# Fewer idle TensorE products at both ends of a Conformer block, and a new order of its blocks and PSUM banks

## The chip, the cores and the metric

One core of a Trainium2 chip runs the whole program. The metric is the device time of one execution in microseconds; three executions are taken and their median counts.

## The reference

A Conformer block over `x` of 2 x 4000 x 144 in bfloat16, with 4 heads of 36:

```python
h = layernorm(x);  x = x + 0.5 * (silu(h @ w_ff1a) @ w_ff1b)       # 144 -> 576 -> 144
h = layernorm(x);  q, k, v = split(h @ w_qkv)                      # 4 heads of 36
x = x + softmax(q @ k.T / 6) @ v @ w_o                             # over all 4000 keys
h = layernorm(x) @ w_pw1;  h = h[:, :144] * sigmoid(h[:, 144:])
x = x + silu(depthwise_conv5(h)) @ w_pw2                           # 5 taps along time
h = layernorm(x);  x = x + 0.5 * (silu(h @ w_ff2a) @ w_ff2b)
return layernorm(x)
```

## The kernel before

The 8000 tokens are cut into 16 chunks of 500, eight per sequence; a chunk is four blocks of 125 tokens. For each chunk of queries the keys come in 63 tiles of 64. A tile's scores (`PS<-QT,KT`, four products of 500 columns) go to two PSUM banks, ScalarE exponentiates both in one instruction (`PT<-PS`, 128 x 1000), and four products `PS<-PT,VA` add the result to banks 6 and 7. Some tiles are exponentiated on VectorE by integer arithmetic instead. Around this stream go, for each chunk, the first feed-forward, the projections, and after attention the output projection, the gated convolution and the second feed-forward. In the middle of the program a sigmoid or silu is a tanh on ScalarE (`TH`) and a product on VectorE (`HT`, `U`, `SW`); in the front and in the tail silu is taken directly. A layer norm is statistics on VectorE (`ST`), a power -0.5 on GpSimd (`RS<-RS,NHALF`), and the scaling (`XN`) on GpSimd in the middle and on VectorE at both ends. Normed rows are transposed to `XT` or `XTQ` by DMAs through memory in the middle, and by TensorE products with `IDENT` and a copy at both ends.

Three stages matter for reading the profile. The front runs chunk 0 in two halves (`pre_first`) up to the first exponential, with chunk 1 beside it. In the middle, attention of all chunks runs against the rest. The tail begins when the last tile of chunk 15 is exponentiated: chunk 15's attention is finished (`epilogue`, copies to `QT`, products with `IDF`, `AN`), and then it and what is left of chunks 11 to 14 go through `post1`, `post2` and the last layer norm (`store`), in halves of 250 tokens.

The program is made in two steps. Generators ask for work and a planner (`Sched`, `pick_any`) emits instructions through `Rec.op`, with planned durations, which fixes what is computed and in which tile. Then `reorder` permutes the blocks of each engine by the table `ORDER`, one character per block (how far the block is shifted in its engine's queue), and `place` takes each PSUM tile's bank from `PLACES`. Semaphores are set after that. Each engine runs its queue strictly in this order.

An idle product is a 128 x 128 product of the identity with itself into bank 7 (`warm`). The program starts with `NWARM = 50` of them. Further ones are put in by `Rec.op`: in the front up to the first exponential, and in the tail, when the planner finds that a TensorE instruction will wait for another engine, it fills the planned wait:

```python
            for _ in range(int((ready - start - 0.12) / 0.056)):
                self.filler()
```

They belong to the block of the instruction that waits, and move with it. Nine such waits of the front got 5, 2, 5, 29, 6, 1, 5, 2 and 1 of them, five of the tail 6, 14, 6, 15 and 9. All instructions are issued by one helper, so every row of the profile has line L377; rows are told apart by their tiles.

Of the kernel before, what the change touches and what calls it, by code (L numbers as in the profile page):

```python
# [32 lines left out]

ALPHABET = '!#$%&()*+,-./0123456789:;<=>?@ABCDEFGHIJKLMNOPQRSTUVWXYZ[]^_`abcdefghijklmnopqrstuvwxyz{|}~'
ORDER = {
    "pe": (
        "PPPPPPPPQOPPPRRRNLPPQSPROQQQHTOPPMRPRMQNV[NZMMMtMKPMOLIOOOQNQORRNTYLVESPPKLRPEEOOOQNPP[PNQNNQOMPP^PP"
        "JPNPNQ[TLNKMQOKPNSQMNUOOOROSPPQXRGNPROUQYHKNNPNPNQQMPPPQOPWXNNNNPMM]]MNNOMQNLQLMMPPPTOOOOPPPQOUOOOOO"
        "TWQWQKLJQNRPWITNNVOLLOORNOQOSYNNPMZNNNOMOOVN[PMSJPLQKQSQWQXHRWRVQRYWRHXR=BRALJRTMVOLWTLMPMPUUHOWORLO"
        "VOOROOBPPQOUPQMPRUQRTLQTQDPIPPQQQQQUQQHMRVOLRNNNPPPTOOOOPPPPQOROQRVOVPQMNPTROWQSLOUNOPXOUROMVMNZOS-R"  # L40
        "MKMOOOQOPQXQOLOOOOOXOOOPNOOOXOOOPNQNTMTOMNXNPNP_OLNQOLRNNN]OMRMOUKVMNYQMRPQHTYCMOLOWOMNNOROQLQOPTOOO"
        "ORROQLPVOOOOOUNOPPQQKPPPPPPPROSPRLTMTNNNOROOUORNORLORPQQSKO[_PYQRNOIFINLTLNNQNPSSNTMMYQNRRSMMSNUOCUP"
        "NYOVPROOJORRTNS>NNPTTOMNNUOOORNNTOOOOXROQSPPSQGXPPPPVOOOTROUSPPUQGPP3PPPQOPPPQRNOSOPXPPQOPVPQRPKBWSO"
        "OQNJOPZPNRNNNQQ]MQOQHPMSPPMKPPPPP^UOOPKMQRLQLRLNVPXMNNQMMTNNROMQQNURNOWRPMIQNNPPRRSNPKPPPPQQNPPPPPUP"
        "PPPQYIOOOOTNNOMRPRRVSPLXNSSMNTUOTJNTRMR8MPQSSOLQQTKQNNSPVMQMNOQNTQSMRNRJOUOOPNOQTNPSSLYLMRRMM]PNQIPM"
        "ORTMSOKQJSSSOSVJRPHPKPQOQOUPNOOQNPQRNOPPSOPNSOSQSQKRPRSOFRRMRMOSQSMRRKMRPNRUSMOTKMPTM_TRLMNQOPRSQMMW"
        "TOOOORO:VPNOOOOPQOPQOQOPROOPPPVOPQOWKPUOKOOVQOIOOOPPPPSOSOPRUQQHLXPPPQOVP_FLNNTMPNWZMPMGLMUMPNLOPQOP"
        "QOPQQURTNJOTROINSOOOQOTOOOQXMOOOPXMNNOOOOOPROOPPQOPPPPPPPPQOPPPPQSPUWQWIKPWJPJQVPQRKSNRfNPPQSSMNNb8R"
        "MMMRLMSMNQSLUN_ZOKNPN>TOLLMRLNQOSQOMPROURPNWO_HNNNNPPLOYNPRRKKPKSPMRN`RMQMMRSMMQNVVNVPXLNPRR@NSVO[NO"
        "OSNOVPMPNPTROSQSZROSQT(EOTJMOSQSNSJNSSPLULOO]NPMWNOOPKMNVMOOSNUMTLNNSMOTXMNNNOPNO]PNOTQNLMNOOORTQMMO"  # L50
        "PQRPSPPQUSGPTQQWQQUQTNCCMRPYPLOOSOOLRMOPPQ]QMNQOWOKNOMNRPRVJNRPMMQOURTMNLNSPSQLWROURPVZQTQTRW?ERAQGQ"
        "QQWPPPPPUBQULMVPNKQNNROOPPVPPXLPYRKOJOROOVPPEOPNPPeRORLOPTOPNUQMNCNNORNQMQQNRRNSQRNUQHQULPLSNPZPK[NO"
        "MPNRKNPKQNPPXOOSNNOMOPVOOOOPNROOPPPPQOPPPPQQNWPPPPPPTHPNOUOROMNQOROOSOPNPQOPQOQOSO`NP[LNOQLYQKPSINSP"
        "RFFPQQNQOPQOPQOUPPPPTPSOOQRPTWQNNWOP;MOOOPVOOOOOXNOO[PMOTTMOHLMO]OOOQNNOSPPMKQOPPSSOOLPPPPSPPQLPPPPQ"
        "OWOWNPMMNNQQRLOPPPPROOPQOPPPPQOPPPTPPSOUOIVNNNYNTMPNOXOWGOWPPULPIEQQLPURNQNSKOOPQOROOPWOQOQOPQVPUFNO"
        "WN_JNNNNNOOQNNOSNPQQQJPXOUNOOOSWMOGVORLNLQRMSPPLPPPRPSMOORPSQOKROOQUPTZOO_RPNEGNOSLNNNOU]MNNNNOPNXOP"
        "LMOPNOPQOPPVOOQOMWNRRMMULNSNOQLQOPRXOPQOPQOG[OOOOOPNTNNNNPQXNOOPPMXQRSXPSLRWEEORPHdLOPQOLcVNLOPTOSHJ"
        "NL[DNOMQMQOKPQRLWPTLNPNLPQOPPP]TOMUNLOLOMOOPPPPPQOSUPMQOKPPROQRPTROINQQQSXKOMOOOOOP]OOQNNOOUNNNO]LQN"
        "NOOOOO]NNQMNUNNNNNNRPNSOOOPWOOOOOTNNOOWOOOOOOOPPPPROSNOQSPLOYOOOTNNOWNPURHOLVKOXPNLPPPROQQGPQOPQQNQQ"
        "QQQKQQWURYZMTQMESHOLCQORSUSOKKQSLPQMQUNRNNRPUQJNURNSKMNRTNVRcMTINRSNSFNO[FOQLMMSOLXMMPVMPMMPTLXUMMQL"  # L60
        "MVLXMNOMRUNNJORNOPQSSXOMJPPPXKPM[PMOOROU_GXKLMVJMMMMTLTLMTMPMOZOOSNNOMOOOPPPRRTTTPNRSTRFNQTAOPNQOPTO"
        "OPNPPQOPPPPPQQRSQRRIWQTQTTEVKVRJRNRKYPP>WNOMNNNRNSNOOQOPZPNVNPPLPKQLP]ROMNOTQNLQNRSVNGNOOOPQOQTRMNRP"
        "YPJPQUNPNOQGWPRMOVLOPSKNSMOOQOPSOOTRMOMPTRPNRPVQOPQOUPUXNQMSQK:RLRROVKQRPLSKOOPSOPRPLPPPPPUOPNOOPPPP"
        "UOPQMRMOQXPMQNNQNNPQOPPPXQNQMNPNRNOPSPNVNOOOOTPPUSPMOTPTUUNLSMNSPP:YOOOQQMMPNPUSNOMRRLUROKNSQRSKPKRO"
        "OVOUNNNNQQLQQNQQQQLSOOOPPSOOYTOLNWPLUKMPRUSQOIRPDQOQOPPRROMPROOQQN"
    ),
    "act": (
        "PPPPPPPPPPPPQRSMNOPRPQQQKPPQOPQOPUOOOOOPPPRPQSQUNIVSSNORIIPPPPPPPPPPPPPQOPPQOPPPPPPPPQOPPPPPPPPPPPPP"
        "PPQOPPPPPPPPPPPPPPPPPPPPPPPPPPPPPPPPPPPPPPPPPPPPPPPPPPPPQOPPPPPPPPPPPPROOROQNPQOPPPPPPPPPPPPPPPPPQOP"
        "QQNPPQOPPPPPPPPPPPPPPPPPPPPPPPPPPQOPPQOPPPPPPPPPPPPROOPPPPPPPPPPPPPPPPPPQOPPPPPPPPPPPPPPPPPPPQOPPPPP"  # L70
        "PQOQOPPPPPPPPQOPPPPPPPPPPPPPPPPPPPPPPQOPPPPPPPPPPPPPPPPPROQNQQQMQOPPPPPPPPPPPQOPPPPPPPPQOPPPPPPPPPPP"
        "PPPPPPPPPPPPPPPPPSOOOPPPPPPPPPQOPPPPPPPPPPPPPPPPPPPQQNPPPPPPPPPPQQNPPQOPPQOPQOQOPPPPPPPPPPPPPPPPPPPP"
        "PPPPPPPPPPQOPPPPPPPPPPPPPPPPPPPPPPPPPPQOPPQOPPPPPPQOPPPPPPPPPPQOPPPPPPPPPPPPPPPPPPPPPPPPPPQOPQOPPPPP"
        "QOQOPPQOPPPQOPPPPPPPPPPPPPPPPPPPPPPPPPPPPPPPQQNPPPPPQOPPPPPPPPPPPPPPPPPPQOPPPPPPPPPPPPPPPPPPPPPPPPPP"
        "PPPPPPPPPPPPPPPPPPPPPQOPPPPPPPPPQOPPPPPPPPPPPPPPPPPPPPPPPPPPPPPPPPPPPPPPPPPPPPPPPPPPPPPPPPPPPPPPPPPQ"
        "OQOQOPPPPPPPPPPPPPPPPPPPPPPPPPPPPPPPPPPPPPPPPPPPPPPPPPPPPPPPPPQOPPPPPPPPPPROOPPQOPPPPPPPPPPQOPPPQOPP"
        "PPPPPPPPPPPQOPPPPPPQOPPPPPPPPPPPPPPQQNPPPPPPPPPPPQOPQOPPPPPPQOPPPPPPPPPPPPPPPPPPPPPPPPPPPPPPPPPPPQOP"
        "PPPPPPPPPPPPPPPPPQOPPPPPPQOQOPPPPPPPQOPQOQOPPPPQOPPQQQMPPPPTOOUQMMOUVMORSSMIJPPPPPQQQMPPPPPPQO"
    ),
    "dve": (  # L80
        "PPQOQQQMPPQOaOOOOQR`MNJNOPLRNNYYHPMKOPJRNQJQQNRROQQQQIUPUPNSSSTGSSSTFSFRSSURUICZJSLOLPVOPNIXNNORNNPM"
        "QQNPQOPQOPPPROOPPPPQOPPPPPPPQOQOPPPQRPQRPQQTPQRRSLPRRTRURUQRURRSTRSWSQRUQUUPQTT#US2T3NSQpTROORPQR?OC"
        "SOMRPQmQINPGMNNNNNNOMPNOOOPNPPPPPPSQSNPQXPPQRRMRMR9QNQOPQOPPPPPPPPPPWPNPNOPNPRRNTPLPQQTPQORPVPPPPP@P"
        "PPQOPQOPROOROQNROOROOcOOOOOOOPNQNNOOOOOOQOQQVMVPNOKNOQOPPSTTOSOJQRHQSQTRPUUWQSGCKKOPPPPPUPTPPRVIPPPR"
        "ORTRNRNSP=WNPNOPNOPUQNPRLNPPPPP_OPNOQNPPLO]NNOMOOPNOOSQMQLQOPPQRNRNQNVPQOQOJPPPQOPPPQOTOTOOLOQQQQQSS"
        "PSSPKRPBRPNPPPQOPQOPPPPQQNPQSNRNQTQOPVQOFOTOMOOQOQQNQQRROQRIRNQXQRNRRMRURRORHRROQ<QRPRROJSPRSQKQQQTP"
        "SOOaRBNNQNNPNOPNOOOOQOROOROOPPQOQOTOOOO_OOPRPLPPPROOGQNPQQNPZPNPQMNPPPLPPPPQOPPPPPPQQNPPPQOPPPQOPTRO"
        "SQSQSJPFPPPROOUQOPPQUQTNORDMQOQOPQQNQSPSLNOPQOPPPPQRPTRKRRRKTPSORRMRPSPTQNRSQSQTJP5O`PPPPPPPPPPEOOPN"
        "PROOQOQOQOPPQOQOQOPQOPPPSPPQLPQRNRNSNPNPROOQOPQQRMOQOPPPPPPPPPPPROOPQSPPQQQIPPPPPPROOPPPRPNTPNPQQLPP"
        "PPROOPRPNQRNOPROOQOQQNROOPPQOQRNQQMQOQQNQQNPPQOPPPQOPRORPMPSOOOQOQOPQUPPUOOPPQSQDNSOOOPPPPPPQQRPRPRP"  # L90
        "RPREORPNPPPSOOOPROQNPPPPPPPROOQQNQOPPQOPPPPPQRNOQQNPPPPPPPPPPQQRMRPSLOUNTQMMMPPPPPPPPPPPPPPPPPPPPPPP"
        "PPROQQQLQTNOOOPPPPPQOQOUPQMPQLPROQRMSNSNNOPPPPPPPPPPPPUPNQNNSOOOPPYOOOOOOOOOQOPRORSQRMQIPPPPRRRMRLOP"
        "PPPPPQOPPPPPPPQOQOROOROQNPPPPPQOQOPPPPPPPPPPPPPPPPPPQOQOPQOPPPQOPROOPPPSOOOPPPPPQOPPPROQTMSORLSLOOPQ"
        "OPPP_OQOROKROLSMNNNPPPPPPPPPPPPQUQMPPRPRPQGPSOORNOPQOQOTPNPSPLOQOSQNTMOPNRROMQOSQRMRLQNPQOPPPPPQQQSQ"
        "SNROQQEPPPPPPPPWPPPQOPRPQFQOPPPPPPQOQOPPPPTQSMMNPPPQRNOSOSOMQRMSNUOMSNRMRLQNQRNOQOQQNPPRSOSOPRRRRTLQ"
        "SQAQQRPHPPQOPPROOROOPPSOOSPPQQQQQQSPPRTRN?NPPPROSNPSPPQTRSNRRLCRPQMPROQNPROQNPPPRRNNPPQOPPUOQOROQXPH"
        "PNOOYbTLNOOXPSPUQQSACFQRUSUSTBUWZQR^SSKCMBO=OPPMORSTNQXQQHPPQOF"
    ),
    "pool": (
        "PQQQQSSOORPQTQOPQQTQQNQQQQQRRORPQQQQQ,PXOOOOOOO_NORNSMMNNOOQNNPWSNNOMPQQQKTTNNNNQQNPPPROTPMTOPTKNROQ"  # L100
        "QKPWOOOOOPNPQOPPSOOQNPPQOPQQN"
    ),
    "sp": (
        "PPPPPPPPQOPPPPPPPPPPPROQSMRNNPPPPPPPPPPPQOQOPPPPWOVNNNNNNPPPPPPRRNNRRNNPPPPPPPPRRNNPPZOOXNOMNNNNNVOO"
        "OO[NNWNNNNNNNNT[NNNNOOOOVNNXMNNNOOOOP[OOPNOOOPPPLPPPQO"
    ),
}
PLACES = (
    "5024031421242530124140023035304230343105232504015043214352103245041522040241204124012401314032034023"
# [40 lines left out]
class Rec:  # L150
# [22 lines left out]
    def op(self, eng, name, *a, r=(), w=(), q=None, cost=0.1, kind=None, lat=None, acc=None, bub=(0.0, 0.0), **k):  # L173
# [27 lines left out]
        start = ready = self.free[eng]  # L201
# [3 lines left out]
        if eng == "pe" and self.filler is not None and not self.filling:  # L205
            self.filling = True
            start = max(start, self.filler_free())
            for _ in range(int((ready - start - 0.12) / 0.056)):
                self.filler()
# [197 lines left out]
class Banks(Slots):  # L407
# [7 lines left out]
    keep = 0  # L415
# [1655 lines left out]
```

## Time and profile before

| | |
|---|---|
| median of three executions | 887.04 us (886.72 to 887.05) |
| the profiled execution | 887.44 us, span 885.6 us from the first to the last instruction |
| ScalarE, TensorE, VectorE, GpSimd busy | 851.5, 857.2, 818.4, 303.9 us |
| first exponential starts | 19.75 us |
| last exponential ends | 847.36 us |
| last TensorE instruction, last VectorE instruction end | 878.6 us, 881.1 us |
| DMA | 28.8 MB, mean 33 GB/s |

Each engine has a queue of its own, and times are from the span's start. In the timeline, `x4` is a run of four like instructions merged into one row with the start of the first and the time to the end of the last; the bracket gives the idle time before it and what ended it. A TensorE product's end is modelled and includes its way through the array (some 0.17 us), so the next row starts before the end of the last. PEld is the loading of weights. `L377` is the helper that issues everything.

### The profile page before, as it was taken

To read this page: it belongs to the slowest core of one execution; us is meant where nothing else is said; L and a number is where in the kernel's file an instruction comes from. 1 tells how busy PE (TensorE), PEld (TensorE's weight loads), DVE (VectorE), ACT (ScalarE), POOL (GpSimd) and SP (SyncE) were. 2 spreads that over 40 slices of the span, in tenths; PEclk is the share of its full clock that TensorE was granted. 3 is DMA by queue.
4 is the path that set the end of the run, shared out by engine and by line. 5 is a ranking of instruction groups with operands and counts; after the bars stand their busy time and mean duration, and the time that the engine had idled before them with its cause. 6 is when DMAs were issued, how large, how long until landed. Compare 5 with 4: busy or idle time off the path is not lost.

```text
span 885.6 us, 27130 instructions
## 1 busy us (share of the span) xinstructions
PE 857.2 (97%) x11478; PEld 385.1 (43%) x11478; DVE 818.4 (92%) x1799; ACT 851.5 (96%) x1095; POOL 303.9 (34%) x584
## 2 busy tenths in 40 slices
PE   8999999999999999999999999999999999999996
PEld 7544333444444434344344444443434343444466
DVE  7968999999999999999988899997988999999987
ACT  6799999999999999999999999999999999999974
POOL 7761500216235235024107125241631017022733
PEclk9999999999999999999999999999999999999999
DMA  4231011112211111212101111002011001101101
GB/s 101 45 61 36 23 37 31 34 23 44 44 30 23 37 30 27 47 24 43 23 19 28 30 32 29 22 17 51 22 37 24 7 15 45 29 9 36 37 17 34
DMA packets 114222, 28.81 MB, mean 33 GB/s; under 512 B 101085, under 2 KB 114100, under 8 KB 114100
## 3 DMA queue, kind: packets, MB, share of 16 engines
q1 hardware_dynamic: 112642, 26.46, 13.7%
q8 instruction: 90, 1.47, 0.7%
q10 hardware_dynamic: 1458, 0.62, 0.3%
q14 instruction: 32, 0.26, 0.1%
HBM read 13.44 MB, written 13.61 MB: 31 GB/s over the span
## 4 chain that ended last, share of the span: by engine, by line
ACT 43%; PE 39%; DVE 14%; POOL 1%; DMA 1%; SPq 1%; issue 1%; DVEq 0%; POOLq 0%
ACT PT L377 39%; PE PS L377 39%; DVE PT L377 8%; ACT TH L377 4%; DVE ST L377 1%; DVE HT L377 1%; DVE X L377 1%; POOL XN L377 1%; DVE QT L377 1%; DVE XN L377 1%; DVE KT L377 1%; SPq L377 1%; DMA XTQ<-rows 1%; POOL RS L377 0%; DVE VA L377 0%
## 5 line engine op out<-in xcount | busy, mean ns | idle before, releaser
L377 ACT ACTIVATE PT<-PS 128x1000 bf16<-128x1000 f32 (+1 forms) x822 | 756.3, 1066 | 5.0 <-PE PS L377 3.8
L377 PE MATMUL PS<-QT,KT 64*64 64x500 bf16 x3968 | 425.6, 385 | 14.0 <-ACT PT L377 8.3
L377 PE MATMUL PS<-PT,VA 64*37 64x500 bf16 x4712 | 410.8, 372 | 2.0 <-DVE PT L377 0.7
L377 DVE TENSOR_SCALAR PT<-PS 128x500 int16<-128x500 f32 x372 | 244.6, 669 | 8.0 <-PE PS L377 6.5
L377 PEld LDWEIGHTS PS<-QT,KT 64*64 64x64 bf16 x3968 | 124.5, 104 | 240.3 <-ACT PT L377 135.5
L377 POOL TENSOR_SCALAR RS<-ST 125x4 f32<-125x4 f32 x130 | 35.2, 271 | 459.9 <-DVE ST L377 453.7
L377 PEld LDWEIGHTS PS<-PT,VA 64*37 64x37 bf16 x4712 | 141.2, 96 | 96.4 <-DVE PT L377 20.7
L377 POOL TENSOR_SCALAR XN<-X,RS 125x144 bf16<-125x144 bf16 x260 | 153.0, 622 | 8.0 <-DMA out_dram<-XN 1.3
L377 DVE TENSOR_SCALAR PT<-PT 128x1000 uint16<-128x1000 uint16 x372 | 150.6, 416 | 1.9 <-PE PS L377 0.5
L377 DVE TENSOR_TENSOR PT<-PT 128x1000 bf16<-128x1000 bf16 x186 | 126.5, 682 | 1.4
L377 ACT ACTIVATE TH<-PS 128x500 bf16<-128x500 f32 (+3 forms) x198 | 105.1, 554 | 4.0 <-PE PS L377 2.7
L377 POOL TENSOR_TENSOR RS<-RS,NHALF 125x4 f32<-125x4 f32 (+1 forms) x93 | 91.5, 987 | 36.2 <-DVE RS L377 30.4
L377 DVE SCALAR_TENSOR_TENSOR HT<-TH,PS 128x500 bf16<-128x500 bf16 (+1 forms) x135 | 80.8, 617 | 17.7 <-ACT TH L377 16.9
L377 PE MATMUL PS<-XT,WA 128*128 128x500 bf16 (+4 forms) x288 | 74.9, 365 | 0.4 <-DVE AN L377 0.2
L377 DVE BATCH_NORM_STATS2 ST<-X 125x6 f32<-125x288 bf16 x160 | 65.6, 446 | 3.1 <-DMA X<-in_x_dram 2.9
L377 DVE SCALAR_TENSOR_TENSOR X<-PS,X 125x288 bf16<-125x288 f32 (+1 forms) x128 | 57.2, 451 | 9.7 <-PE PS L377 8.6
L377 PE MATMUL PS<-WB,HT 128*125 128x144 bf16 (+1 forms) x640 | 51.9, 230 | 0.6 <-ACT HT L377 0.4
L377 PEld LDWEIGHTS PS<-WB,HT 128*125 128x125 bf16 (+1 forms) x640 | 44.2, 136 | 14.0 <-issue 4.6
L377 POOL COPY U<-U 128x2 bf16<-128x2 bf16 (+1 forms) x54 | 12.0, 260 | 71.4 <-DVE U L377 71.4
L377 PEld LDWEIGHTS PS<-XT,WA 128*128 128x128 bf16 (+1 forms) x288 | 21.2, 97 | 34.0 <-issue 12.5
L377 PE MATMUL PS<-U,DG 128*128 128x375 bf16 (+6 forms) x204 | 29.0, 264 | 0.2 <-DVE PT L377 0.2
L377 DVE STREAM_TRANSPOSE XN<-XN 128x320 f32<-128x320 f32 x54 | 27.0, 500 | 1.7 <-POOL XN L377 1.6
(93 smaller groups left out, 533.3 us busy)
## 6 DMA issues: line engine op xcount, KB each, us to landing
rows<-XN SPq DMA_DIRECT2D x216, 40.0 KB, 2.0
XT<-rows SPq DMA_DIRECT2D x56, 128.0 KB, 2.0
rows<-AN SPq DMA_DIRECT2D x60, 40.0 KB, 2.0
X<-in_x_dram SPq DMA_DIRECT2D x16, 140.6 KB
XTQ<-rows SPq DMA_DIRECT2D x26, 70.3 KB
out_dram<-XN SPq DMA_DIRECT2D x13, 140.6 KB
XT<-rows SPq DMA_DIRECT2D x56, 16.0 KB, 1.9
out_dram<-XN SPq DMA_DIRECT2D x3, 70.3 KB
```

The lines of the kernel that those rows point to most:

```text
L377: ins = getattr(eng, o.name)(*o.a, **o.k)
```

## The change

`Rec.op` keeps at most `FILLS[n]` idle products in the n-th wait that it fills. The planner's clocks go on as if all were there, so the planned program has the same instructions otherwise. The front keeps 31 of 56 (12 of 29, 3 of 6 and 3 of 5, and none of the last two), the tail none of 50; the 50 at the start stay. The tables `ORDER` and `PLACES` are replaced. Apart from the idle products every engine has the same instructions. 185 of 1720 PSUM tiles get another bank; on TensorE 6989 of 11322 products, and on VectorE 920 of 1799 instructions, have another place in the queue, mostly by a few places; ScalarE's 1103 change by at most four.

```diff
+FILLS = (5, 2, 5, 12, 3, 1, 3, 0, 0, 0, 0, 0, 0, 0)
+
 ORDER = {
     "pe": (
-        "PPPPPPPPQOPPPRRRNLPPQSPROQQQHTOPPMRPRMQNV[NZMMMtMKPMOLIOOOQNQORRNTYLVESPPKLRPEEOOOQNPP[PNQNNQOMPP^PP"
+        "PPPPPPQOQOPPPPPRPNPQRSOPKQQQMTOOPNQOQQQM|]NbMMMrLLQMMMHHLNLMOLQNPRVGSIOSQHHQSGHLMMOOPPZPNQNNQOMPbPPQ"
...
 PLACES = (
-    "5024031421242530124140023035304230343105232504015043214352103245041522040241204124012401314032034023"
+    "5304235415231501253015424035304230043214020532141052312043340552105410450241204124012401314032034023"
...
@@ Rec.__init__
         self.filling = False
+        self.calls = 0
@@ Rec.op
         if eng == "pe" and self.filler is not None and not self.filling:
             self.filling = True
             start = max(start, self.filler_free())
-            for _ in range(int((ready - start - 0.12) / 0.056)):
-                self.filler()
+            n = int((ready - start - 0.12) / 0.056)
+            if n > 0:
+                self.calls += 1
+                keep = min(n, FILLS[self.calls - 1])
+                for _ in range(keep):
+                    self.filler()
+                if keep < n:
+                    if self.kind != "f":
+                        start += self.SWITCH + (0.006 if self.kind == "q" else 0.0)
+                    self.kind = "f"
+                    self.free[eng] = (self.free[eng] if keep else start) + (n - keep) * 0.056
             self.filling = False
             start = self.free[eng]
```

In the tail the new order has, among others, the two `WP2` products of chunk 14 ahead of the transposes of chunk 15's first half, `glu_end` of chunk 15's first half ahead of chunk 13's transposes, and the convolution of chunk 15's first half ahead of two of chunk 13's feed-forward tiles. In the front the products `PS<-XTQ,WK` of chunk 0's first half stand ahead of chunk 1's second transposes, and VectorE's first two memsets ahead of the first statistics.

## The prediction

> **What bounds the kernel now.** I read the page first, then the busy time by stage, then the chain of work that ended last, and at the end the timeline around the idle products. The page has three engines near full:
>
> ```profile
> PE 857.2 (97%) x11478; PEld 385.1 (43%) x11478; DVE 818.4 (92%) x1799; ACT 851.5 (96%) x1095; POOL 303.9 (34%) x584
> ```
>
> An average says little here, so I cut the span at the first exponential (19.75 us), the end of the opening (45), the end of the last exponential (847.36), a turn of the chain (858.78) and the last VectorE instruction (881.10). Columns: stretch, length, then busy time and count of PE, PEld, DVE, ACT, POOL, then clock and DMA.
>
> ```profile
> 0.00:19.75 19.75, 17.97 (x226) 15.66 (x226) 13.98 (x57) 11.79 (x27) 14.22 (x43) 1.00 0.44 109
> 19.75:45.00 25.25, 23.92 (x248) 13.23 (x248) 24.30 (x66) 20.71 (x37) 19.99 (x40) 1.00 0.22 45
> 45.00:847.36 802.36, 784.84 (x10633) 329.72 (x10630) 748.95 (x1571) 797.74 (x980) 257.94 (x487) 1.00 0.14 30
> 847.36:858.78 11.42, 10.67 (x110) 7.82 (x108) 10.63 (x32) 8.56 (x19) 2.20 (x3) 1.00 0.13 27
> 858.78:881.10 22.32, 19.78 (x268) 18.68 (x268) 20.53 (x78) 12.71 (x34) 9.59 (x13) 1.00 0.07 21
> ```
>
> From 45 to 847 us ScalarE is busy 797.74 of 802.36: 4.62 us is all that an order can win there while ScalarE's work is the same. From 19.75 to 45 TensorE (1.33 idle) and VectorE (0.95 idle) are the limits. In the tail VectorE is: it idles 0.79 + 1.79 = 2.58 of 33.74. The chain says something else of the tail:
>
> ```profile
> 858.78 14.97 PE PS L377 x207
> 873.75 0.03 issue
> 873.77 0.46 DVE X L377
> ```
>
> Fifteen unbroken microseconds of TensorE. But idle products are in them, and an idle product makes TensorE look busy while it waits. The timeline shows which:
>
> ```profile
> 860.13 1.18 ACT L377 ACTIVATE XT<-PS 128x250 bf16<-128x250 bf16 x4 [0.90 <-PE PS L377]
> ...
> 861.32 0.94 PE L377 MATMUL PS<-IDENT 128*128 128x128 bf16 x14
> 862.10 0.60 PE L377 MATMUL PS<-XT,WA 128*128 128x250 bf16 x4
> ...
> 868.71 0.50 PE L377 MATMUL PS<-IDENT 128*128 128x128 bf16 x6
> 869.05 0.79 PE L377 MATMUL PS<-WB,HT 128*125 128x144 bf16 x10
> ...
> 869.72 0.54 DVE L377 TENSOR_SCALAR XN<-X,ST,RS 125x144 bf16<-125x144 bf16 x2
> ...
> 869.89 1.00 PE L377 MATMUL PS<-IDENT 128*128 128x128 bf16 x15
> 870.73 0.39 PE L377 MATMUL PS<-IDENT,XN 125*128 125x125 bf16 x4
> ```
>
> The 14 run to 862.10, though the XT that the next product reads was copied by 860.13 + 1.18 = 861.31. The front has the same picture:
>
> ```profile
> 1.53 5.36 PE L377 MATMUL PS<-IDENT 128*128 128x128 bf16 x50 [1.53 <-POOL NHALF L377]
> ...
> 12.23 1.78 PE L377 MATMUL PS<-IDENT 128*128 128x128 bf16 x29
> 13.85 0.39 PE L377 MATMUL PS<-IDENT,XN 125*72 125x125 bf16 x4
> ...
> 12.87 0.54 DVE L377 TENSOR_SCALAR XN<-X,ST,RS 125x144 bf16<-125x144 bf16 x2
> ```
>
> XN is there at 13.41, its transposes start at 13.85. A product follows its input by some 0.04 us (HT ends 858.74, the product starts 858.78).
>
> **The sum, part by part.** An idle product costs (13.85 - 12.23) / 29 = 0.056 us of TensorE's queue. The 75 are 4.2 us of it, but only what runs past the awaited input can be won.
>
> Tail, by groups. The 14: next input 861.31, start 862.10, so 0.75 won. The 6 at 868.71: HT ends at 868.88 (ScalarE's 868.02 row lasts 0.86), start 869.05, so 0.13. The 15: XN at 870.26, start 870.73, so 0.43. These three lie inside the chain's TensorE piece: 1.31. The 6 at 857.54 hold XN of 857.06 to 857.88 (0.34), but the chain is on ScalarE there; the 9 at 877.24 end at 877.74, with HT at 877.67 (0.03); both at nothing. Next late is VectorE. Of its 1.79 idle after 858.78, 0.82 (at 859.91) and 0.20 (at 867.14) wait for TensorE and 0.30 for a tanh behind it: 1.3 at most. The new order puts the two WP2 products of chunk 14 ahead of chunk 15's first transposes; they are what VectorE awaits at 859.91. Bounds: 0 (each wait comes back elsewhere) and 1.8 (all of VectorE's idle). I take 1.1, nearer to the 1.31, since VectorE must still be kept fed.
>
> Front. The 17 fewer of the 29 free 0.40 us before chunk 0's first XTQ transposes, but the first exponential hangs on the second half: its XN comes at 15.27 + 0.62 = 15.89, after GpSimd's three powers (13.04 to 15.21), whose order is kept. Its transposes now start at 16.07, after 5 idle products; 3 would let go at 15.94. From there the queue to the first scores has three idle products less (2 and 1, 0.17), but one tanh more stands ahead of ScalarE's first exponential. VA's copy (19.41) changes places with a small op that reads 0.86; the second scores' wait of 0.45 us for VA can fall by up to 0.35. Bounds 0 and 0.8; I take 0.4. The two VectorE memsets moved ahead of the first statistics (0.20 + 0.16) go into its 2.94 us wait for X: nothing; without that cover 0.36.
>
> 19.75 to 45: blocks of chunks 1 and 2 change places. Bounds: minus 0.9 (VectorE's idle) and plus 1.5, a third of ScalarE's 4.54 idle there once more; I take minus 0.2.
>
> 45 to 847: in the two built programs, idle products left out, 414 of the 814 score pairs that ScalarE exponentiates have as many products ahead of them as before; 804 are moved by 8 or fewer (8 at 0.053, from 4 in 0.21 us, is 0.43 us). ScalarE's own order is nearly the same. GpSimd's and SP's blocks move too, where GpSimd is busy 32%. ScalarE's waits of 0.15 us and over there sum to 2.5 us. Bounds: minus 2.5 and plus 6.4 (the rival below). I take minus 0.4, a small share, as pairs move both ways.
>
> Sum: 1.1 + 0.4 + 0.2 + 0.4 = 2.1. The profiled execution took 887.44 (span 885.6 and 1.84 around it), 0.40 above the median of 887.04. It becomes 885.3, and the median 884.9.
>
> The clock. The first 50 products take (6.86 - 1.53) / 50 = 107 ns each, later ones 56: TensorE starts at half speed and leaves it after some 5.3 us of work. The clock column reads 1.00 all the while, so only a duration shows it. With few idle products TensorE has pauses: after the change some 1.1 of the 3.7 us from 12.23 to 15.94, and in the tail some 7%, much as in 847 to 858 now (0.75 of 11.42), where products run at full speed. I put it at nothing; a new warm-up costs 50 x 0.051 = 2.5 us. The Trainium skill, TensorE: Matmul & The Clock Gate, Part 1, says that an idle window of about 3.4 us halves the clock; no pause here is that long. The same page, A second HAM failure mode, speaks against the change: short pauses between groups of products can make the clock go back and forth. By the first rule the sum stays 884.9; by the second it is the last rival. The pauses of 0.45, 0.25 and 0.40 us at 20 to 24 us, with scores of 0.38 to 0.41 per four around them, speak for the first.
>
> **Rivals.**
> 1. The order wins more: half of ScalarE's 4.54 idle from 19.75 to 45 goes. For it: it is the largest idle of the busiest engine. Against: TensorE and VectorE are 95% busy there. 884.9 - 2.1 = 882.8, with 0.2 of it already counted.
> 2. Nothing to speak of: the removed products only covered waits, since VectorE is 92% busy in the tail. Then 0.3 in the tail, 0.2 in front: 886.5.
> 3. Slower, by ScalarE starving between 45 and 847. About 150 score pairs have 4 to 12 more products ahead. Each 4 are 0.21 us; if one pair in five is not covered, 30 x 0.21 = 6.4 us are lost: 887.04 - 1.7 + 6.4 = 891.7. It decides from 8 pairs on, where 1.7 is used up. For it: ScalarE has 0.6% slack. Against: a pair usually waits for ScalarE, as TensorE's commonest wait is for it (8.9 us).
> 4. Slower by the clock: one warm-up in the front, where the pauses would be 30%, and one in the tail: 5.0, so 890.3.
>
> **How the numbers follow.** Forecast 0.40, with its own range 883.5 to 885.3; rival 1 0.14, 2 0.20, 3 0.20, 4 0.06. A measurement tells 0.2% (1.77 us) from no change, so faster is 0.40 + 0.14 = 0.54, same 0.20, slower 0.26. The range of 882.0 to 891.5 leaves out about half of rival 3's upper side and a little of rival 1.
>
> **What would show it.** Right: TensorE's first product after chunk 13's XT copies follows them by under 0.1 us; VectorE idles under 1.6 us from the last exponential to its end; the first exponential starts 0.1 to 0.5 earlier; ScalarE's idle from 45 us to the last exponential stays at 3.5 to 5. Wrong: that idle at 7 or more (rival 3), products of 107 ns after the front (rival 4), or a tail no shorter than 38 us (rival 2).

## The result, and the profile after

The changed kernel takes 888.22 us, the median of 22 executions (886.70 to 893.54); the kernel before, beside it, 887.19 (22 executions, 886.72 to 887.85). The ratio is 1.0015, with a 95% interval of 1.0008 to 1.0021: slower by 0.15%, where 884.9 was forecast. A second series of 11 gave 887.71 against 887.29, 1.0012 (0.9999 to 1.0025). Two executions of the series below, a kernel before at 1295.22 us and one of experiment 9 at 1927.65, were far slower than all others and no ratio counts them.

The median hides what is new: the kernel before stays within 1.1 us, the changed one spreads over 6.8. Over both series its 33 executions fall into groups by their mean granted clock:

| mean clock | executions | time, median and range (us) |
|---|---|---|
| 0.997, 0.998 | 14 | 887.2 (886.7 to 887.7) |
| 0.996 | 8 | 888.2 (887.6 to 888.5) |
| 0.992 to 0.995 | 9 | 889.6 (888.8 to 890.7) |
| 0.989, 0.987 | 2 | 894.1, 893.5 |

So there are two things to explain: why the best group is not at 884.9, and what the other 19 executions have lost. The profiled execution is of the best group: 887.22 us, span 885.4. Its page has the same load on each engine as before:

```profile
PE 853.1 (96%) x11403; PEld 379.9 (43%) x11403; DVE 817.7 (92%) x1799; ACT 850.8 (96%) x1095; POOL 300.0 (34%) x584
```

Busy time by stage, cut at the first exponential (19.85), 45 us and the end of the last exponential (847.83); columns as before:

```profile
19.85:45.00 25.15, 23.64 (x240) 12.52 (x240) 24.23 (x65) 20.70 (x38) 20.00 (x40) 1.00 0.18 39
45.00:847.83 802.83, 783.76 (x10640) 329.02 (x10637) 749.59 (x1571) 797.51 (x980) 253.57 (x482) 1.00 0.14 31
847.83:881.05 33.22, 28.51 (x328) 23.72 (x326) 30.20 (x109) 21.02 (x52) 12.24 (x20) 1.00 0.10 25
```

In the middle ScalarE's idle time is 802.83 - 797.51 = 5.32 us, 0.70 more than before. The tail, from the last exponential to VectorE's last instruction at 880.94, is 33.10, 0.7 less. The first exponential is 0.10 later. The whole loss of the middle is in one place; no other 50 us of the two traces differ like this one. First before, then after:

```profile
95.00:145.00 50.00, 47.84 (x687) 17.55 (x686) 48.93 (x111) 49.82 (x58) 9.92 (x18) 1.00 0.11 24
```

```profile
95.00:145.00 50.00, 45.58 (x663) 17.36 (x666) 48.21 (x106) 47.63 (x55) 10.98 (x18) 1.00 0.11 23
```

ScalarE, 49.82 of 50 us busy before, loses 2.2. The timeline of after shows how:

```profile
99.44 0.47 DVE L390 TENSOR_SCALAR PT<-PT 128x1000 uint16<-128x1000 uint16 x1
...
100.20 2.23 POOL L390 MEMSET AN<- 128x2560 bf16 x1
...
100.69 2.58 DVE L390 TENSOR_SCALAR PT<-PT 128x1000 uint16<-128x1000 uint16 x1
...
102.37 0.63 POOL L390 MEMSET U<- 128x640 bf16 x1
...
103.32 0.61 PE L390 MATMUL PS<-PT,VA 64*37 64x500 bf16 x8 [2.11 <-DVE PT L390]
...
104.19 1.00 ACT L390 ACTIVATE PT<-PS 128x1000 bf16<-128x1000 f32 x1 [1.95 <-PE PS L390]
```

A step of VectorE's integer exponent (`PT<-PT`, 128 x 1000 uint16), 0.41 us as a rule, takes 2.58. It starts while GpSimd clears `AN` and ends 0.27 us after GpSimd has cleared `U`. TensorE waits 2.11 for it, and the scores queued behind come 1.95 late for ScalarE. The two memsets are one GpSimd block, the first of `setup_dw`. The new table puts it behind four layer-norm groups that stood after it. Before, it ran beside two copies out of PSUM and a transposition of `XN` on VectorE, and nothing was held; each took its usual time:

```profile
58.90 2.24 POOL L377 MEMSET AN<- 128x2560 bf16 x1
...
59.42 0.68 DVE L377 CAST KT<-PS 128x500 bf16<-128x500 f32 x1 [0.61 <-PE PS L377]
...
60.02 0.50 DVE L377 STREAM_TRANSPOSE XN<-XN 128x320 f32<-128x320 f32 x1
...
60.44 0.64 DVE L377 CAST KT<-PS 128x500 bf16<-128x500 f32 x1
```

The Trainium skill, SBUF — State Buffer, section "SBUF: two separate sides", has the rule: GpSimd and VectorE share a pair of ports, which is locked, not divided, so that "the other fully blocks"; of VectorE it names operations in a two-port mode, and some with two inputs in SBUF, not all. The trace agrees: 2.58 us for an operation of 0.41, and no hold on the three operations of before. That the exponent step runs in a two-port mode no trace here shows.

### The profile page after: what moved, and what is told of

Its sections match the earlier page's. It is cut to its first block, busy times and chain, and to the rows that moved or that the text cites. A ratio compares the mean times of both kernels' runs of the same rounds, so it can differ in the third digit from the quotient of the medians.

```text
span 885.4 us, 26988 instructions
## 1 busy us (share of the span) xinstructions
PE 853.1 (96%) x11403; PEld 379.9 (43%) x11403; DVE 817.7 (92%) x1799; ACT 850.8 (96%) x1095; POOL 300.0 (34%) x584
## 3 DMA queue, kind: packets, MB, share of 16 engines
q8 instruction: 89, 1.46, 0.7%
## 4 chain that ended last, share of the span: by engine, by line
ACT 44%; PE 35%; DVE 19%; issue 1%; DMA 0%; SPq 0%; POOL 0%; DVEq 0%; POOLq 0%
ACT PT L390 39%; PE PS L390 35%; DVE PT L390 11%; ACT TH L390 4%; DVE HT L390 2%; DVE X L390 1%; DVE ST L390 1%; DVE XN L390 1%; DVE QT L390 1%; DVE KT L390 1%; DVE AN L390 0%; DMA XT<-rows 0%; SPq L390 0%; ACT XT L390 0%; DVE U L390 0%
## 5 line engine op out<-in xcount | busy, mean ns | idle before, releaser
L390 DVE TENSOR_SCALAR PT<-PT 128x1000 uint16<-128x1000 uint16 x372 | 153.6, 423 | 1.9 <-PE PS L390 0.7
L390 POOL TENSOR_SCALAR XN<-X,RS 125x144 bf16<-125x144 bf16 x260 | 148.2, 602 | 6.8
L390 ACT ACTIVATE TH<-PS 128x500 bf16<-128x500 f32 (+3 forms) x198 | 107.1, 560 | 7.2 <-PE PS L390 5.9
L390 PE MATMUL PS<-XT,WA 128*128 128x500 bf16 (+5 forms) x288 | 74.7, 365 | 1.2 <-DMA XT<-rows 0.6
```

Source lines behind the costliest of these rows:

```text
L390: ins = getattr(eng, o.name)(*o.a, **o.k)
```

## The experiments

Beside each run ran the kernel before, at 887.22 to 887.38 in the three series. The theory after the traces was M: the moved memset costs 2 us. For the spread there was C: without idle products TensorE loses its clock in some executions.

**1. The memsets back at their old place.**

```diff
-        "PQQQQRSOPRPQTQOPQQSPROQQQQQQQSPPQQQQQ,PXOOOOOOO...
+        "PQQQQRSOPRPQTQOPQQSPROQQQQQRROQQQQQQQ,PXOOOOOOO...
```

> The changed kernel with one edit: the block of two GpSimd memsets (AN, U) goes back ahead of the four layer-norm groups that the new order put before it, to where the kernel before has it (58.9 us). Theory M (the memset holds VectorE's second exponent operation: 2.58 us at 100.69 instead of 0.41, and ScalarE waits 1.95 us for it): no such operation over 0.9 us is left, ScalarE's busy time from 95 to 145 us goes from 47.6 back to about 49.8, the last exponential ends at 845.9 instead of 847.8, and the median falls by 2.0 from 888.2 to 886.2. Theory C (the missing idle products cost clock in some executions): the executions spread over several us as much as the changed kernel's (886.7 to 893.5) and the lowest mean clock stays under 0.996. Rival (the wait comes back elsewhere, since ScalarE is then held by the next chunk's scores): the median stays within 0.5 of 888.2.

Measured: 885.26 (11 executions, 884.66 to 886.97), ratio 0.9977 (0.9969 to 0.9986), 2.1 us faster than the kernel before. By stage:

```profile
45.00:845.40 800.40, 783.13 (x10636) 328.23 (x10633) 746.75 (x1570) 796.91 (x980) 254.29 (x482) 1.00 0.14 31
```

ScalarE idles 3.49 in the middle, the last exponential ends at 845.40, and the exponent step next to the old stall takes 0.41. M holds. But the spread went too: one execution at clock 0.995, ten within 1.0 us. Theory C said that it would stay. Where that one execution lost its clock no profile shows.

**2 to 4. Idle products put back in the changed kernel**: all 75, the tail's 50, the front's 25.

```diff
-FILLS = (5, 2, 5, 12, 3, 1, 3, 0, 0, 0, 0, 0, 0, 0)
+FILLS = (5, 2, 5, 29, 6, 1, 5, 2, 1, 6, 14, 6, 15, 9)     # 2
+FILLS = (5, 2, 5, 12, 3, 1, 3, 0, 0, 6, 14, 6, 15, 9)     # 3
+FILLS = (5, 2, 5, 29, 6, 1, 5, 2, 1, 0, 0, 0, 0, 0)       # 4
```

> The changed kernel with all 75 idle products put back in their blocks, the new order and banks kept. Theory C: the mean granted clock is 0.998 or more in every execution, highest minus lowest is about 1.1 us as in the kernel before, and the median is 887.3 (the changed kernel's executions at clock 0.997 are 886.7 to 887.7, and the tail's idle products add up to 0.66). Theory M alone: the spread has nothing to do with idle products, the median is 888.2 or up to 0.7 more, and executions above 889 remain. The wait of ScalarE at 104 us (1.95) is there in both.

> The changed kernel with the tail's 50 idle products put back, the front's 25 left out. Theory C with the loss in the tail: all executions within 1.2 us, clock 0.998 or more, median 887.3. Theory C with the loss in the front: the spread stays as in the changed kernel (several executions above 889 with clock 0.995 and less), median 888.2 to 888.9. If the clock plays no part: same as the last.

> The changed kernel with the front's 25 idle products put back, the tail's 50 left out. Theory C with the loss in the front: all executions within 1.2 us, each with a mean clock of 0.997 (the end of the span, where TensorE has no work, lowers it), median 887.0. Theory C with the loss in the tail: the spread stays (executions above 889 with clock 0.995 and less), median 888.2.

Measured: 892.69 (6 executions, clock 0.988 to 0.994), 891.56 (5, three of them at 0.993 or 0.994), 890.24 (12, seven at 0.995 or less). M alone misses the time too, with 888.2 to 888.9 for experiment 2; what the idle products add is taken up below. Theory C falls, front and tail alike: with every idle product back, the clock is lost in all six executions. The profiles of 2 and 3 show where. Here is 2, cut at the moments at which its clock changes (the last three columns are clock, DMA share, GB/s):

```profile
100.69:104.10 3.41, 1.45 (x24) 0.44 (x16) 3.38 (x3) 2.46 (x3) 3.23 (x3) 1.00 0.09 27
104.10:107.51 3.41, 3.26 (x19) 0.72 (x20) 2.82 (x7) 1.26 (x2) 1.25 (x2) 0.50 0.00 0
107.51:110.92 3.41, 3.41 (x24) 0.81 (x22) 1.72 (x5) 2.25 (x3) 2.78 (x6) 0.50 0.00 0
110.92:114.34 3.42, 3.37 (x71) 1.53 (x71) 2.74 (x8) 3.14 (x4) 0.00 (x0) 1.00 0.00 0
```

TensorE's clock falls to half just after the memset's stall and stays there for 6.83 us. So one cause has two prices: the pause that the memset makes, and, in executions in which the clock reacts to it, half speed after it. The fall lasts 6.83 us in 2 and 3 (and 3.41 in experiment 12), and just ahead of it lies a stretch of 3.41 that holds most of the pause, with 1.45, 1.30 and 1.79 of products. The Trainium skill, TensorE: Matmul & The Clock Gate, Part 1, says that activity is judged in free-running windows of 3413 ns, which don't start with the kernel. The traces agree: in 2 the clock first rises at 5.11 us, falls 29 such windows later at 104.10, comes back two later and falls again, behind the last product, 227 after that. Over the fourteen profiles the first rise lies between 4.56 and 7.15 us, so the windows' edges fall at other places in each execution, and the same pause falls into one window or is cut in two. In the profiles of 4 and 8, whose clock stayed up in the middle, an edge cuts it: 2.30 and 2.42 us of products in the two windows in 4, 2.28 and 2.33 in 8.

The second finding of these runs is the tail: 35.4 us with the idle products, 33.1 without. That is the next question.

**5 to 7. The parts by themselves**: the old order without the tail's idle products, the old order with the front's 25 left out, and the new order (memsets back) with all 75.

```diff
 # 5, 6: tables of the kernel before; 7: tables of experiment 1
+FILLS = (5, 2, 5, 29, 6, 1, 5, 2, 1, 0, 0, 0, 0, 0)       # 5
+FILLS = (5, 2, 5, 12, 3, 1, 3, 0, 0, 6, 14, 6, 15, 9)     # 6
+FILLS = (5, 2, 5, 29, 6, 1, 5, 2, 1, 6, 14, 6, 15, 9)     # 7
```

> The kernel before (its order and banks) with the tail's 50 idle products left out and nothing else. Theory I (the prediction's term: 1.31 us of TensorE overshoot in three groups, VectorE next late): the time from the last exponential's end to VectorE's last instruction goes from 33.8 to about 32.7, and the median from 887.4 to 886.3. Theory O (in the old order VectorE is late at the same places, and it is the new order that makes room): 33.6 to 33.8 us, median 887.2 to 887.4. If idle products are what keeps the clock up in the tail, the time goes up by over 1 and products of 107 ns appear there.

> The kernel before with 25 of the front's 56 idle products left out and nothing else. Prediction's term: the first exponential starts 0.1 to 0.4 us before 19.75, median 887.0 to 887.3. Rival (the start of chunk 0's second half hangs on GpSimd's powers, and the start varies by as much with the moment at which the clock goes up, 5 to 7 us): first exponential within 0.1 of 19.75, median 887.4.

> The new order and banks with the two GpSimd memsets back at their old place and all 75 idle products put back: what order and banks are worth by themselves. By the runs with the memset at 100 us (tail 35.4 us with idle products and 33.1 without, first exponential at 20.1 with the front's and 19.8 without): tail 35.4, median 885.3 + 2.3 + 0.3 = 887.9, every mean clock at 0.998 or more. If idle products cost clock by themselves in the new order: mean clocks of 0.994 and less remain and the median is 890 or more.

Measured: 886.79 (0.9996, 0.9987 to 1.0005), 887.57 (1.0002, 0.9993 to 1.0011) and 888.35 (1.0011, 1.0002 to 1.0020). The tail, in us, from the profiles (before, 5, 7 and 1; from the last exponential's own end, by which before has 33.79 where the prediction's cut gave 33.74):

| | with idle products | without |
|---|---|---|
| old order | 33.79 | 33.45 |
| new order | 35.35 | 33.12 |

Neither part is worth much alone: leaving out gives 0.34 (33.45 is nearer to theory O's 33.6 to 33.8 than to theory I's 32.7), reordering costs 1.56. Together they give 0.67. The timelines show why. That of 7 has, among others:

```profile
857.80 0.50 PE L390 MATMUL PS<-IDENT 128*128 128x128 bf16 x6
...
860.83 0.94 PE L390 MATMUL PS<-IDENT 128*128 128x128 bf16 x14
```

That of after has the same stretch without them:

```profile
860.11 0.38 PE L390 MATMUL PS<-IDENT,XN 125*128 125x125 bf16 x4
860.33 0.79 PE L390 MATMUL PS<-WB,HT 128*125 128x144 bf16 x10
...
860.95 0.39 PE L390 MATMUL PS<-IDENT,XN 125*128 125x125 bf16 x4
861.22 0.61 PE L390 MATMUL PS<-XT,WP 128*128 128x250 bf16 x4
```

In the new order real products follow each other from 860.11 to the end of TensorE's work, with no pause over 0.1 us. Hardly a wait is left for idle products to fill, so they push the rest back: 35.35 - 33.12 = 2.23 us for 50, or 0.045 each of their 0.056. In the old order they lie in waits, and VectorE's idle time in the tail moves by 0.10 only when they go (2.61 to 2.51).

The front has the same pattern. In the old order the first exponential starts at 19.54 to 19.76 us, with the front's 25 idle products or without them (four profiles). In the new order it starts at 19.93 to 20.19 with them (2, 4 and 7) and at 19.39 to 19.86 without (seven profiles), 0.45 earlier in the mean. So experiment 2 adds up: the best group's 887.2, 2.4 for the clock (the table's third group), 2.2 for the tail and 0.45 for the front make 892.3, and 892.69 was measured.

The mean clock is 0.997 or more in every execution of 5, 6 and 7: with or without idle products at the ends, none of these 33 executions, which have no stall in the middle, lost it. The one execution of experiment 1 at 0.995 stays unexplained.

**8, 9. The memset in pieces**: at its new place in four instructions of 128 x 640; or one half there and the other half ahead of the four groups.

```diff
-        op("pool", "memset", ANS[:, :, :], 0.0, w=[("AN", a) for a in range(NAN)], cost=2.2)
+        for a in range(NAN):                                                   # 8
+            op("pool", "memset", ANS[:, a, :], 0.0, w=[("AN", a)], cost=2.2 / NAN)
+        op("pool", "memset", ANS[:, 0:2, :], 0.0, w=[("AN", 0), ("AN", 1)], cost=1.1)   # 9
+        op("pool", "memset", ANS[:, 2:4, :], 0.0, w=[("AN", 2), ("AN", 3)], cost=1.1)
+        pool.insert(i - 29, pool.pop(i))                                       # 9, the second half
```

> The changed kernel, the GpSimd memset of AN at its new place (100.2 us) but in four instructions of 128 x 640 instead of one of 128 x 2560. Theory M in its narrow form (VectorE is kept out for as long as one GpSimd instruction lasts): VectorE's exponent operation is held for at most one piece (0.6 us, so some 1.0 instead of 2.58), ScalarE's wait behind it is under 0.6 instead of 1.95, no execution has the clock halved at 104 us, and the median is 885.5 to 886.2. Rival (GpSimd keeps the port over back-to-back instructions, as long as its queue is full): VectorE's operation still takes 2.4 or more, and the median stays at 888.2.

> The changed kernel with one half of the AN memset (128 x 1280) moved ahead of the four layer-norm groups and the other half left at 100 us. VectorE was held until both memsets (AN 2.23, U 0.63) were over, in one piece or in four. If the hold lasts as long as GpSimd's memsets go on: 2.58 becomes about 1.5, ScalarE's wait of 1.95 becomes about 0.9, the median is 1.1 under the changed kernel's executions with clock 0.997 (887.0), so 885.9. If TensorE's clock falls only after a window of 3.4 us that is less than some 45% busy (the pause here is 1.0 and leaves 65% or more), no execution has a clock under 0.996 and all lie within 1.5 us. If the clock falls at any pause of a microsecond, executions with 0.994 remain.

Measured: 8 gives 888.68, ratio 1.0018 (1.0009 to 1.0027), clock down to 0.992, no better than one piece; 9 gives 886.20, ratio 0.9986 (0.9977 to 0.9995), every clock 0.997 or more. First 8, then 9:

```profile
99.58 2.34 POOL L390 MEMSET AN<- 128x640 bf16 x4
...
100.08 2.69 DVE L390 TENSOR_SCALAR PT<-PT 128x1000 uint16<-128x1000 uint16 x1
...
101.87 0.63 POOL L390 MEMSET U<- 128x640 bf16 x1
```

```profile
100.59 1.16 POOL L394 MEMSET AN<- 128x1280 bf16 x1
...
101.08 1.51 DVE L394 TENSOR_SCALAR PT<-PT 128x1000 uint16<-128x1000 uint16 x1
...
101.69 0.63 POOL L394 MEMSET U<- 128x640 bf16 x1
...
102.65 0.60 PE L394 MATMUL PS<-PT,VA 64*37 64x500 bf16 x8 [1.04 <-DVE PT L394]
```

In its narrow form M was wrong: the step is let in when the last of GpSimd's memsets in a row is done, and ends 0.27 us after `U` in all three kernels; it is not let in between two of them. With less to clear, the hold is shorter, the pause 1.04, and the clock stays up.

**10. The pause filled.** The changed kernel with 32 idle products into a free bank during the pause.

```diff
@@ before R.reorder(ORDER)
+    spare = R.place(99, 1)[0]
+    for _ in range(32):
+        warm(bk=spare)
@@ reorder: ahead of the products that wait for the held step
+        lines["pe"] = rest[:1217] + pads + rest[1217:]
```

> The changed kernel with 32 idle products put into TensorE's pause behind the held exponent operation (1.8 of 2.11 us, into a bank that is free there). It takes the clock's part from the memset's: VectorE is still held 2.58, ScalarE still waits 1.95. If the clock's fall is what sets executions of 888 to 891 apart from those of 886.7 to 887.3: no execution has the clock halved in the middle, all lie within 1.5 us, median 886.9. If the spread has another cause: executions above 889 remain and the median is 888.2 as before.

Measured: 887.12 (886.41 to 888.06), ratio 0.9998 (0.9989 to 1.0007), every clock 0.997 or more.

```profile
100.32 2.58 DVE L394 TENSOR_SCALAR PT<-PT 128x1000 uint16<-128x1000 uint16 x1
...
101.03 1.96 PE L394 MATMUL PS<-IDENT 128*128 128x128 bf16 x32 [0.19 <-ACT PT L394]
...
103.82 1.90 ACT L394 ACTIVATE PT<-PS 128x1000 bf16<-128x1000 f32 x2 [1.95 <-PE PS L394]
```

The hold and ScalarE's wait are the same to the hundredth, yet the groups of lower clock are gone. This takes the two prices apart: the clock cost the median of all 33 executions 888.1 - 887.1 = 1.0 us, the hold 887.12 - 885.26 = 1.9.

**11. The same move in the old order.** Only the memsets of the kernel before, moved behind the four groups.

```diff
-        "PQQQQSSOORPQTQOPQQTQQNQQQQQRRORPQQQQQ,PXOOOOOOO...
+        "PQQQQSSOORPQTQOPQQTQQNQQQQQQQSQOQQQQQ,PXOOOOOOO...
```

> The kernel before with only the two memsets moved behind the same four layer-norm groups (in the old order the fourth ends at 101.9 us, so the memsets run from there to 104.7). VectorE's next exponent operation is due at 103.4. Theory M: it is held until about 104.8, some 1.3 us; ScalarE loses about 0.7 to 1.3 and the median is 888.0 to 888.7, with TensorE's pause too short for the clock, so no clock under 0.996. If GpSimd meets none of VectorE's exponent operations there: 887.3, nothing held.

Measured: 892.12 (6 executions, 889.28 to 895.17), ratio 1.0052 (1.0033 to 1.0072). The step was held 2.52, not 1.3: VectorE reached it at 102.24, a microsecond earlier than expected, just after the memset had begun at 101.70. TensorE paused 1.72, and four of six executions lost clock, where none was expected to. Two at 0.998 stand at 889.3, 2.0 over the kernel before: the price of the hold alone, again. One moved block is enough to make the kernel slower by more than the whole change brings.

**12. The changed kernel again.**

> The changed kernel again, beside the other three. By its executions so far (9 of 22 at 888.7 or more): median 887.2 to 889, some executions with clock 0.995 or less. If the profiled one is among these, the clock is 0.5 for two windows of 3.41 us from the end of the window that holds most of the pause at 101 us, and the scores take 0.63 per four instead of 0.41 there, as in the two profiles with idle products.

Its times are in the table at the top. This time the profiled execution (888.53, clock 0.996) was one that had lost clock:

```profile
101.88:105.29 3.41, 1.79 (x19) 0.58 (x20) 3.41 (x6) 1.46 (x3) 1.29 (x2) 1.00 0.00 0
105.29:108.70 3.41, 3.41 (x24) 0.81 (x22) 2.51 (x7) 2.41 (x4) 3.00 (x7) 0.50 0.03 5
```

and the scores take 0.63 us per four in the second row's time, against 0.41 before and after:

```profile
104.78 0.41 PE L390 MATMUL PS<-QT,KT 64*64 64x500 bf16 x4
...
105.92 0.63 PE L390 MATMUL PS<-QT,KT 64*64 64x500 bf16 x4
...
108.93 0.41 PE L390 MATMUL PS<-QT,KT 64*64 64x500 bf16 x4
```

One window of half speed here, two in experiment 2 and 3. One is 3.41 x 0.5 / 886 = 0.0019 of the mean clock, two are 0.0038, so they stand for the groups at 0.996 and, roughly, at 0.992 to 0.995 (the profiles have 0.996 with one window, 0.993 and 0.994 with two). By the table they cost 1.0 and 2.4 us. The two executions under 0.990 would by the same estimate need about five windows; no profile fell on such a one, so what happens there stays open.

## Why the prediction was wrong

Its sum was 2.1 us and its time 884.9. With the memsets put back the same change takes 885.26, 2.1 under the kernel before. The sum thus holds for all of the change but one block, but that is in part luck: the tail gave less than its term, the middle's order more, and the front's 0.36 is within the scatter of single profiles (below). In us, against before:

| term | predicted | after | memsets back |
|---|---|---|---|
| first exponential | -0.4 | +0.10 | -0.36 |
| ScalarE's idle time from there to 45 us | -0.2 | -0.09 | -0.10 |
| ScalarE's idle time from 45 to the last exponential | -0.4 | +0.70 | -1.13 |
| tail | -1.1 | -0.7 | -0.7 |

**The step that failed** is the one for 45 to 847 us: "GpSimd's and SP's blocks move too, where GpSimd is busy 32%". It read an engine's low load as a free move. What the block was, how long it lasts (2.24 and 0.64 us stood in the trace of before) and which VectorE operation would then run beside it was not asked. The order of the two programs showed it: the one long memset of the middle, put from a stretch in which VectorE has no exponent step into one of exponent steps. The same sign, on a small scale, stood in the front of the trace of before, in the operation of which the prediction says that it "reads 0.86":

```profile
19.06 0.86 DVE L377 TENSOR_SCALAR RS<-ST 125x2 f32<-125x2 f32 x1
...
19.37 0.53 POOL L377 MEMSET XT<- 80x512 bf16 x1
```

Its median in that trace is 0.16; here it ends 0.02 after a GpSimd memset. The 0.86 was used and not asked about. That it is the same hold is likely, but no run tests it.

The bounds of the failed term, minus 2.5 to plus 6.4, held the result, but by another mechanism: rival 3 had score pairs later by products ahead of them, and its sign, ScalarE idle for 7 us or more, did not come (5.32).

**The clock.** The prediction put it at nothing, as no pause would be as long as 3.4 us, and rival 4 placed a loss in the front and the tail. The pause that mattered was in the middle, 2.11 us long, and enough. The sentence on the idle window was read too strictly: the pause need not be 3.4 us long, if a window holds too little work (1.30 to 1.79 us of products in 3.41). Of rival 4 the mechanism came true, in another place, at 1.0 or 2.4 us and in 19 of 33 executions; in none of the fourteen profiles did front or tail lose the clock, once it was up, before TensorE's work was over. (Rival 4's 890.3 is 0.4 more than 884.9 + 5.0, and the prediction does not say why.) The short pauses between groups of products did nothing that the runs show: experiments 5, 6 and 10 have them in front or tail at a clock of 0.997 or more. So of the two rules that the prediction took from the Trainium skill, TensorE: Matmul & The Clock Gate, the one of Part 1 was the one that mattered, and the second failure mode did not show, unless the one slow-clocked execution of experiment 1 was such a case.

**The tail** was mis-sized. The 1.31 us of overshoot were counted on the old order. There, leaving out gives 0.34, close to rival 2's 0.3, since VectorE is late next, as the prediction feared. The order was treated as a help to that; in truth it is a change of the bound, from VectorE's waits to an unbroken TensorE queue, which is worth something only without idle products. Of the signs, TensorE's first product after chunk 13's `XT` copies came as forecast: they end at 862.17 + 0.65, it starts at 862.87, 0.05 behind. VectorE's idle time in the tail did not fall under 1.6; it is 2.90. The wait at 859.91 that was to go (0.82) has become

```profile
860.04 0.46 DVE L390 SCALAR_TENSOR_TENSOR X<-PS,X 125x288 bf16<-125x288 f32 x1 [1.28 <-PE PS L390]
```

because the `WP2` products that VectorE awaits have themselves to wait 0.42 for ScalarE's `HT` (at 859.56). The tail to the span's end, 38 us or more by rival 2, is 37.6.

**The front** gave nothing by itself: experiment 6 starts the first exponential at 19.71 instead of 19.75. The first half's transposes start 0.31 earlier, the second half's 0.07, for they wait for their `XN`; this the prediction had seen, and it then counted 0.17 behind it, which did not come. With the new order the start is 19.62 in the mean of seven profiles, against 19.69 in the four of the old order: 0.07, where 0.4 was taken. Among the seven it lies anywhere from 19.39 to 19.86, so a single profile can't show a term of 0.4. The prediction's 5.3 us of work before full speed is no constant either: the first 50 products take 4.39 to 5.51 us over the fourteen profiles, as the clock goes up at another moment each time.

**The middle's order** was undersized: experiment 1 takes 1.13 us out of ScalarE's 4.62 of idle time, a quarter, where a tenth was taken (experiment 7, with the same order, takes out 1.46). A further 0.36 of its earlier end comes from ScalarE's own work, which is that much shorter in this profile; why, is open.

## What to carry to other kernels

A block that moves on an engine with much free time is not free: look up its longest instructions, and what the engines it shares a path with will be doing at the new time. Here GpSimd's long memset belongs where none of VectorE's exponent steps runs beside it, and splitting it into pieces issued in a row didn't help.

Idle products and the order of the real ones are one decision: the tail's 50 cost 0.34 us where TensorE waits and 2.23, most of their length, where it no longer does. And where the spread of a kernel's executions widens, look at the mean clock of each before trusting the median; one stall of two microseconds can be the reason.

## What the runs showed of the hardware that was not expected

- A step of VectorE's exponent is kept out over consecutive GpSimd memsets, not for one: it takes 2.58 us with one piece of `AN`, 2.69 with four, 1.51 with half of it; in each case it is done 0.27 us after the last memset of the row. VectorE as a whole is not kept out: in the trace of before, copies out of PSUM (0.68 and 0.64 us) and a transposition within SBUF (0.50) ran beside the same memset at their usual length. The Trainium skill, SBUF — State Buffer, SBUF: two separate sides, has the lock held "for the whole instruction"; here it outlasts it. GpSimd's scalings (`XN`, 0.50 us each and issued in a row) do not do this: in the trace of before the 65 such steps that lie beside them take 0.45 us in the mean and 0.68 at most.
- TensorE's clock halves after a window with 1.30, 1.45 or 1.79 us of products in 3.41 (experiments 3, 2 and 12). It stayed up after 1.91 in the first profile of after, but also after 1.57 and 1.63 in the tails of before and of experiment 9. So the busy time of the records is not exactly what is judged; somewhere near half a window is the edge. The Trainium skill, TensorE: Matmul & The Clock Gate, Part 1, speaks of an idle window of about 3.4 us; here a pause of 2.11 was enough, and by the mean clocks of experiment 11 one of some 1.7, while one of 1.04 was not.
- After the fall the clock came back after one window (experiment 12) or two (2 and 3), although TensorE was 96 to 100% busy from the first on.
